# The first pair of heads in two half copies, a feature cast on ScalarE and 26 constant matmuls ahead of TensorE's queue

## The chip, the cores and the metric

One Trainium2 chip, one of its cores. The metric is the device time of one launch in microseconds (us), as the median of several runs; less is better. Engines are named as the profile names them: PE (TensorE; PEld for its weight loads), DVE (VectorE), ACT (ScalarE), POOL (GpSimd), SP (SyncE, which here only issues DMAs).

## The reference, cut to what matters

Attention with a feature map, for 8 batches, 8 heads, 576 tokens and a head width of 64, and then a dense mixture of 8 experts:

```
def phi(x):
    proj = np.einsum('bhsd,df->bhsf', x, w_phi)                  # 64 -> 128 features
    proj = proj - np.max(np.abs(proj), axis=-1, keepdims=True)
    return np.concatenate([np.exp(proj), np.exp(-proj)], axis=-1)
q_p, k_p = phi(q), phi(k)
kv  = np.einsum('bhsf,bhsd->bhfd', k_p, v)
num = np.einsum('bhsf,bhfd->bhsd', q_p, kv)
den = np.einsum('bhsf,bhf->bhs', q_p, np.sum(k_p, axis=2))[..., None] + 1e-06
x   = (num / den), as 4608 tokens x 512
P   = 8 rounds of row and column scaling of exp(x @ w_gate)
out = sum over e of P[:, e] * (relu(x @ w1[e]) @ w2[e])
```

The change lies in the first steps of the attention: bringing k and q of the first two heads into the layout in which `phi` is computed.

## The kernel before, in words

**Attention.** Heads are taken in pairs. For a pair, 512 of the 576 tokens are loaded as `acc` tiles (float32, 128 partitions); the remaining 64 tokens of a batch's heads, the "rest", are handled together (`rest_a`). In `pair_a` a pair of an early batch is turned on PE: four 128x128 transposes of k into one bank of PSUM, four of q into another (line 752), and each bank is copied as bfloat16 into the tile `qkT`: k's by DVE (line 756), q's by ACT (line 760). Then `tokens` projects k: four matmuls with 128 tokens each as weights and the feature matrix `wphi2` (256 columns: the 128 features of either head) as the moving operand. DVE takes the maximum of the absolute values (`m`, line 614), ACT the exponentials (`k`, line 618). `feature_rows` projects q the other way round with two matmuls of 512 columns, from which ACT makes `q`; another `tokens` on q yields q's maxima. After that come the sums over tokens (`kv`), numerators and denominators (lines 905 to 919), and the result is turned into `xT` (lines 934 and 937). Batches 0 and 1 are turned on PE, later ones by DMA.

**Experts.** From about 200 us on the rest of the kernel multiplies blocks of `xT` with the experts' weights (lines 1466, 1475, 1607), in an order written out by hand. The change touches nothing there.

**What sets the order of the work.** The kernel records its operations in a `Plan`: `pe(...)`, `act(...)`, `dve(...)`, `pool(...)` and `dma(...)` append one with a rough duration, what it reads and what it writes. `Plan.schedule` then plays all engines forward and gives each the operation that can start first, ties by the order of recording; buffers, among them the eight PSUM banks, are dealt out in that play. What comes out is one fixed list of instructions for each engine, and semaphores between them. An engine never passes over a waiting instruction. Lines 614, 618 and 622 are helpers that record maxima, exponentials and matmuls, so many operations carry these lines.

**The start.** Before the first pair can be projected, `wphi2` must stand: it holds the 64x128 matrix `w_phi` twice, at partitions 0 to 63 for the first head and 64 to 127 for the second, with zeros elsewhere. DVE clears it (line 1042); two DMAs, issued by ACT (lines 1035 and 1037), bring `w_phi` into both halves of `wphi_f`; DVE casts each half to bfloat16 as it lands (line 1044). SP issues the loads of k, q and v of the first pair, of k and q of the second, and of the rest (lines 544, 558 and 600). The tile `colw`, 128x128 ones, is set by DVE (line 1055) and used much later.

Of the kernel before, what the change touches and what calls it, by code (L numbers as in the profile page):

```python
# [349 lines left out]
def kernel(  # L350
# [11 lines left out]
    nc = tc.nc  # L362
# [26 lines left out]
    colw = const.tile([128, 128], BF16, name="colw")  # L389
# [5 lines left out]
    acc = [accp.tile([128, 4, DD], FP32, name=f"acc{g}", tag=f"acc{g}") for g in range(NA)]  # L395
# [3 lines left out]
    identf = a_in.tile([128, 128], FP32, name="identf")  # L399
    wgate_f = a_in.tile([128, NP, E], FP32, name="wgate_f")  # L400
    wphi_f = a_in.tile([128, DF], FP32, name="wphi_f")
    wphi2 = a_in.tile([128, 2, DF], BF16, name="wphi2")
# [10 lines left out]
    def pe(cols, fn, r=(), w=(), takes=()):  # L413
        plan.op("PE", max(cols / 2400.0 + 0.0025, 0.031), 0.22, fn, r, w, takes)

    def act(el, fn, r=(), w=()):
        plan.op("ACT", max(el / 1200.0 + 0.058, 0.107), 0.22, fn, r, w)

    def dve(el, fn, r=(), w=(), shared=False):
        plan.op("DVE", el / 960.0 + 0.07, 0.15, fn, r, w, shared=shared)  # L420

    def pool(el, fn, r=(), w=()):
        plan.op("POOL", el * 1.68e-3 + 0.13, 0.15, fn, r, w, shared=True)
# [4 lines left out]
    def dma(queue, nbytes, rate, fn, r=(), w=()):  # L428

        speed, unit = LINK.get(rate, (rate, 40))  # L430
        if nbytes == 2 << 20:
            speed, unit = 400, 150
        o = plan.op(queue, 0.8 if queue == "POOL" else 0.6, 0.0, fn, r, w, (), nbytes / speed)
        o.turn, o.unit = rate == 148, unit
# [71 lines left out]
    def new(tag):  # L506
        return R[tag].new()
# [28 lines left out]
    def load_qk(b, hh, nh, t, r=()):  # L536

        o = hh % 4
        keys = [o // 2] if nh == 2 else [0, 1]
        if b < 2:  # L540
            g = t["f"]
            for x, src in ((1, k), (0, q)):
                i = 2 * x + o // 2
                dma("SP", nh << 17, 320, lambda x=x, src=src, i=i: nc.sync.dma_start(
                    out=acc[g][:, i:i + nh // 2].rearrange("p a (h c) -> p (a h) c", h=2),
                    in_=src[b, hh:hh + nh, 0:SM].rearrange("h (p j) d -> p h (j d)", j=NJ)),
                    r, [("acc", g, 2 * x + n) for n in keys])
            return
        for x, src in ((1, k), (0, q)):
            dma("POOL", nh << 17, 230, lambda x=x, src=src: nc.gpsimd.dma_start(  # L550
                out=t["qk"]()[:, x, o:o + nh],
                in_=src[b, hh:hh + nh, 0:SM].rearrange("h (p j) d -> p h (j d)", j=NJ)),
                r, [(t["qk"], x, i) for i in keys])
# [67 lines left out]
    def mm(out_, lhsT, rhs, start, stop):  # L621
        nc.tensor.matmul(out_, lhsT=lhsT, rhs=rhs, start=start, stop=stop)  # L622

    def two(merged):

        if merged:
            b = new("P2")
            return [b], [lambda: b()[:, 0:512], lambda: b()[:, 512:1024]]
        b = [new("PP") for _ in range(2)]
        return b, b  # L630

    def tokens(pp, stat, n, r, takes=()):

        if not TI:
            for c in range(n):
                pe(256, lambda c=c: mm(pp[1][2 * c // n]()[:, 1024 // n * c % 512:][:, 0:256],
                                       stat(c), wphi2f, True, True),
                   r + ["wphi2"], [pp[0][2 * c // n * (len(pp[0]) - 1)]], takes)
            return

        def rows():
            for c in range(n):
                for x in range(2):
                    nc.tensor.matmul(pp[1][x]()[:, 128 * c:128 * c + 128],
                                     lhsT=stat(c)[64 * x:64 * x + 64],
                                     rhs=wphi[64 * x:64 * x + 64], start=True, stop=True)

        o = plan.op("PE", n * 0.056, 0.22, rows, r + ["wphi"], pp[0], takes)
        o.tiled = 1
# [18 lines left out]
    def rest_a(b, t):  # L668
# [25 lines left out]
        own = r["E"] + r["T"] + [m, r["r"], r["em"]]  # L694
        pp = two(RM)
        tokens(pp, lambda c: rT()[:, c, :], NP, [rT], own)
        if TI:
            mk = [(m, x) for x in range(2)]
# [43 lines left out]
    def pair_a(b, pr, t):  # L742

        h0 = (2 * pr) % 4
        s = {}
        if b < 2:
            g = t["f"]
            for x in (1, 0):
                ptr = new("PP")
                i = 2 * x + h0 // 2  # L750
                for c in range(4):
                    pe(128, lambda c=c, i=i, ptr=ptr: nc.tensor.transpose(  # L752
                        ptr()[:, c * 128:(c + 1) * 128], acc[g][:, i, c * 128:c * 128 + 128],
                        identf), [("acc", g, i), "identf"], [ptr])
                if x:
                    dve(512, lambda x=x, ptr=ptr: nc.vector.tensor_copy(
                        out=t["T"]()[:, x, 2 * h0:2 * h0 + 4, :].rearrange("p a b -> p (a b)"),
                        in_=ptr()), [ptr], [(t["T"], x, h0 // 2)])
                else:
                    act(512, lambda x=x, ptr=ptr: nc.scalar.copy(  # L760
                        out=t["T"]()[:, x, 2 * h0:2 * h0 + 4, :].rearrange("p a b -> p (a b)"),
                        in_=ptr()), [ptr], [(t["T"], x, h0 // 2)])

        def qkT(x, c, n):

            o = 2 * h0 + c
            return t["T"]()[:, x, o:o + n, :].rearrange("p a b -> p (a b)")
# [7 lines left out]
        own = s["E"] + s["T"] + [s["v"], em, m, s["r"]]  # L775
        at = (0, 2)

        def scores(x, pp):

            merged = (QM, KM)[x]  # L780
            for i, buf in enumerate(pp[0]):
                n = 1 + merged
                if TI or (GR and x == 0):
                    def src(buf=buf, n=n):
                        return buf().rearrange("p (h c f) -> p h c f", h=n, c=4)

                    def part(full, i=i, n=n):
                        return full.rearrange("p (c h) f -> p h c f" if len(full.shape) == 3
                                              else "p (c h) -> p h c", h=2)[:, i:i + n]
                else:  # L790
                    def src(buf=buf, n=n):
                        return buf().rearrange("p (c f) -> p c f", f=DF)

                    def part(full, i=i, n=n):
                        return full[:, 4 * i:4 * i + 4 * n]

                maxes(512 * n, lambda part=part: part(m()[:, at[x]]), src, [buf],
                      [(m, x, i), ("max", x, NP * b + pr)])
                if x == 1:
                    for y, sg in ((0, 1.0), (1, -1.0)):  # L800
                        exp(512 * n, lambda y=y, part=part: part(s["E"][y]()), src, sg,
                            [buf], [(s["E"][y], i)])
            return [(m, x, i) for i in range(2 - merged)]

        pk = two(KM)
        tokens(pk, lambda c: qkT(1, c, 1), 4, [(t["T"], 1, h0 // 2)], own)
        mk = scores(1, pk)
        pool(8, lambda: nc.gpsimd.tensor_scalar_mul(m()[:, 1], m()[:, 2], -1.0), mk, [(m, "neg")])
        exp(16, lambda: em(), lambda: m()[:, 1:3], 1.0, mk + [(m, "neg")], [em])
        pool(1024, lambda: nc.gpsimd.tensor_tensor(  # L810
            out=s["v"]()[:, :, :, 0:D],
# [219 lines left out]
    for b in range(2):  # L1031
# [4 lines left out]
        w=["wphi_f0"])  # L1036
    dma("ACT", 1 << 15, 100, lambda: nc.scalar.dma_start(out=wphi_f[64:128, :], in_=w_phi),
        w=["wphi_f1"])
    load_v(0, 0, 2, halves[0, 0])
    pool(300, lambda: make_identity(nc, identf), w=["identf"])  # L1040
    act(128, lambda: nc.scalar.copy(out=ident, in_=identf), ["identf"], ["ident"])
    dve(128, lambda: nc.vector.memset(wphi2, 0.0), w=["wphi2"])
    for i in range(2):
        dve(64, lambda i=i: nc.vector.tensor_copy(
            out=wphi2[64 * i:64 * i + 64, i, :], in_=wphi_f[64 * i:64 * i + 64, :]),
            [f"wphi_f{i}"], ["wphi2"])
    load_qk(0, 2, 2, halves[0, 0])
    load_rests(0, 1)
    load_v(0, 2, 2, halves[0, 0])
# [2 lines left out]
    for i in range(2):  # L1052
        dve(450, lambda i=i: nc.vector.memset(vrd[i], 0.0),
            w=[("vrd", i, h, *y) for h in range(2) for y in ((), (1,))])
    dve(128, lambda: nc.vector.memset(colw, 1.0), w=["colw"])
    dma("SP", 1 << 14, 50, lambda: nc.sync.dma_start(
        out=wgate_f, in_=moe_w_gate.rearrange("(c p) e -> p c e", p=128)), w=["wgate_f"])
    act(32, lambda: nc.scalar.copy(out=wgate, in_=wgate_f), ["wgate_f"], ["wgate"])
# [4 lines left out]
    def stage_a(i):  # L1063
        b, pr = i // 4, i % 4
        st[i], ms[i], qs[i] = pair_a(b, pr, halves[b, pr // 2])
# [993 lines left out]
```

## Time and profile before

| | |
|---|---|
| three runs | 1010.14, 1010.58, 1012.14 us; median 1010.58 |
| span of the profiled execution | 1008.8 us, 1.8 us less than the median |
| PE busy | 994.0 us |
| DVE busy | 898.6 us |
| ACT busy | 812.8 us |
| POOL busy | 447.6 us |

The span runs from the first to the last instruction of the program in one execution; the runs' times hold what lies around it too, and the profile tells no time of its own beside the span. A matmul's end in the profile is modelled, so the starts of matmuls say more than the sums of their durations. A row of the instructions in order of time has start and length in us, engine, line, operation, what is written from what, and in brackets the engine's idle time before it and what ended it. PEld rows often carry the wait of the matmul behind them.

### The profile page before, as it was taken

How to read it: one execution, taken by the hardware profiler on the slowest of the kernel's cores; microseconds unless marked ns; L12 is line 12 of the kernel's file. 1: busy time of each engine (PE TensorE's matmuls, PEld its weight loads, DVE VectorE, ACT ScalarE, POOL GpSimd, SP SyncE). 2: the span in 40 equal slices, each digit the busy share in tenths (PEclk: the TensorE clock that was granted, in tenths of full speed). 3: DMA queues.
4: the chain of work that ended last, by engine and by line, in shares of the span. 5: the costliest groups of instructions: out<-in, count | busy, mean ns of one | idle time of the engine just before them, and what ended most of it. 6: DMA issues, size and time to landing. Idle time of an engine off the chain costs nothing.

```text
span 1008.8 us, 23309 instructions
## 1 busy us (share of the span) xinstructions
PE 994.0 (99%) x8376; PEld 727.7 (72%) x8376; DVE 898.6 (89%) x1999; ACT 812.8 (81%) x1930; POOL 447.6 (44%) x514
## 2 busy tenths in 40 slices
PE   7899999999999999999999999999999999999998
PEld 5666666644566877777777877787778777787775
DVE  7999998987888998899989898989889988989886
ACT  7999999845979788878878788777887888778874
POOL 5778674400133344434444444444443444344443
PEclk9999999999999999999999999999999999999999
DMA  9999999181136423282327133632246222724653
GB/s 249 183 202 183 157 153 144 38 170 56 53 121 143 147 97 98 84 184 96 109 98 170 44 100 131 130 127 98 97 117 177 97 98 84 147 79 142 208 174 126
DMA packets 129748, 128.86 MB, mean 128 GB/s; under 512 B 55776, under 2 KB 98272, under 8 KB 129632
## 3 DMA queue, kind: packets, MB, share of 16 engines
q1 hardware_dynamic: 97680, 103.33, 36.3%
q0 software_dynamic: 31648, 23.86, 16.9%
q8 instruction: 65, 1.06, 0.5%
q14 instruction: 51, 0.42, 0.2%
q10 hardware_dynamic: 304, 0.20, 0.1%
HBM read 122.50 MB, written 19.53 MB: 141 GB/s over the span
## 4 chain that ended last, share of the span: by engine, by line
PE 92%; DVE 3%; ACT 2%; DMA 2%; issue 1%; POOL 0%; DVEq 0%
PE ps L1466 41%; PE ps L1475 20%; PE ps L622 17%; PE ps L1607 11%; PE ps L905 2%; DMA xi6t<-X 1%; DMA xi<-X 1%; PE ps L752 1%; ACT q L618 0%; DVE m L614 0%; ACT k L618 0%; DVE wx L614 0%; DVE X L1240 0%; DMA acc<-in_k_dram 0%; DVE hs L1676 0%
## 5 line engine op out<-in xcount | busy, mean ns | idle before, releaser
L1875 POOL TENSOR_TENSOR acc<-acc,hx 128x512 f32<-128x512 f32 x186 | 236.1, 1276 | 404.7 <-ACT hx L1872 135.0
L1466 PEld LDWEIGHTS <-hs 128*128 128x128 bf16 x1984 | 194.1, 98 | 46.4 <-issue 0.2
L1872 ACT ACTIVATE hx<-ps,P 128x256 f32<-128x256 f32 x372 | 158.9, 483 | 53.4 <-PE ps L1466 52.0
L1860 DVE SCALAR_TENSOR_TENSOR acc<-ps,P,acc 128x256 f32<-128x256 f32 x372 | 162.2, 478 | 30.2 <-PE ps L1466 28.2
L1475 PE MATMUL ps<-xT,T 128*128 128x512 bf16 x608 | 171.0, 379 | 0.0
L1466 PEld LDWEIGHTS <-hx 128*128 128x128 bf16 x1488 | 145.6, 98 | 24.9
L1466 PE MATMUL ps<-hx,hs 128*128 128x256 bf16 x992 | 144.3, 273 | 0.0
L1676 DVE CUSTOM_DVE_ANT_0 hs<-ps,U 128x512 bf16<-128x512 f32 x192 | 124.7, 684 | 11.3 <-PE ps L1475 6.6
L1607 PE MATMUL ps<-xT 128*128 128x256 bf16 x576 | 125.4, 272 | 0.0
L1475 PEld LDWEIGHTS <-T 128*128 128x128 bf16 x672 | 65.8, 98 | 40.6
L1682 ACT ACTIVATE hs<-ps 128x512 bf16<-128x512 f32 x96 | 55.9, 598 | 41.7 <-PE ps L1475 40.2
L1466 PE MATMUL ps<-wx,hs 128*128 128x256 bf16 x560 | 78.4, 273 | 0.0
L622 PE MATMUL ps<-w,hx 128*128 128x512 bf16 x288 | 73.0, 379 | 0.0
L622 PE MATMUL ps<-xT,w 128*128 128x512 bf16 x288 | 72.9, 379 | 0.0
L1466 PE MATMUL ps<-wx,hx 128*128 128x256 bf16 x496 | 72.3, 273 | 0.0
L1676 DVE CUSTOM_DVE_ANT_0 hs<-ps,X 128x512 bf16<-128x512 f32 x96 | 65.1, 684 | 7.8 <-PE ps L1607 6.9
L1466 PE MATMUL ps<-hx 128*128 128x256 bf16 x496 | 71.2, 273 | 0.0
L1607 PEld LDWEIGHTS <-xT 128*128 128x128 bf16 x576 | 56.3, 98 | 17.5
L1466 PE MATMUL ps<-w,hx 128*128 128x256 bf16 x432 | 62.2, 273 | 0.0
L614 DVE TENSOR_REDUCE m<-ps 128x4 f32<-128x512 f32 x88 | 58.8, 680 | 3.7 <-PE ps L622 1.9
L1672 ACT COPY X<-ps 128x512 f32<-128x512 f32 x96 | 58.6, 610 | 2.5 <-DVE ps L1650 2.5
L1466 PE MATMUL ps<-w,hs 128*128 128x256 bf16 x432 | 60.2, 273 | 0.0
(174 smaller groups left out, 2256.0 us busy)
## 6 DMA issues: line engine op xcount, KB each, us to landing
xT<-xi SPq DMA_DIRECT2D x48, 448.0 KB, 4.6
xT<-xd SPq DMA_DIRECT2D x72, 256.0 KB, 4.0
wx<-in_moe_w_dram POOLq DMA_DIRECT2D x8, 1024.0 KB, 11.2
v_m<-in_v_dram SPq DMA_DIRECT2D x15, 512.0 KB, 5.2
out_dram<-acc SPq DMA_DIRECT2D x14, 512.0 KB, 3.0
w<-in_moe_w_dram POOLq DMA_DIRECT2D x6, 1024.0 KB, 11.0
xT<-xp SPq DMA_DIRECT2D x24, 256.0 KB, 2.8
qk<-in_k_dram POOLq DMA_DIRECT2D x12, 256.0 KB, 5.4
```

What stands on the lines that cost most here:

```text
L614: dve(el, lambda: nc.vector.tensor_reduce(out=dst(), in_=src(), axis=AX.X, op=ALU.max, apply_absolute_value=True), r, w)
L622: nc.tensor.matmul(out_, lhsT=lhsT, rhs=rhs, start=start, stop=stop)
L905: pe(65, lambda j=j: nc.tensor.matmul(pn()[:, j * D1:j * D1 + D1], lhsT=s["T"][x]()[:, j % 2, 2 * h + j // 2, :] if j < 4 else r["T"][x]() ...
L1466: pe(256, lambda i=i, k=k, z=z: nc.tensor.matmul(bank()[:, 256 * i:256 * i + 256], lhsT=lhs(k, i), rhs=rhs(k), start=first and z, stop=k = ...
L1475: pe(512, lambda k=k: nc.tensor.matmul(bank().rearrange("p (a b) -> p a b", a=2), lhsT=lhs(k), rhs=rhs(k), start=first and k == 0, stop=k ...
L1607: pe(256, lambda: nc.tensor.matmul(halves_of(bank[q], n)(), lhsT=lhs(), rhs=t()[:, rhs, :], start=start, stop=True, skip_group_check=True) ...
L1672: act(512, lambda: nc.scalar.copy(out=flat(to[q])(), in_=bank[q]()), [bank[q]], [(to[q], 0), (to[q], 1)])
L1676: dve(515, lambda: nc.vector._custom_dve(ADD_SAT, out=out_(q, i, j), in0=bank[q]().rearrange("p (a b) -> p a b", a=2), in1=to[q](), s0=3.0 ...
L1682: act(512, lambda: nc.scalar.activation(out=out_(q, i, j), in_=bank[q]().rearrange("p (a b) -> p a b", a=2), func=ACT.Relu, bias=0.0, scal ...
L1860: dve(320, lambda n=n, ts=ts: nc.vector.scalar_tensor_tensor(out=acc[g][:, ts, 256 * j:256 * j + 256], in0=bank()[:, 256 * n:256 * n + 256 ...
L1872: act(370, lambda n=n: nc.scalar.activation(out=u()[:, n, :], in_=bank()[:, 256 * n:256 * n + 256], func=ACT.Copy, bias=0.0, scale=P[:, 4 ...
L1875: pool(695, lambda: nc.gpsimd.tensor_tensor(out=acc[g][:, 2 * i:2 * i + 2, 256 * j:256 * j + 256], in0=acc[g][:, 2 * i:2 * i + 2, 256 * j: ...
```

## The change

Three things are done, all in the first 10 us of the kernel.

1. For the first pair of the first batch, k's four transposes go into two banks, two in each. ACT copies the first two as one piece of 256 columns, DVE the last two. The projection of k names the half that it reads. The transposes and the copy of q, and all other pairs, are as before.
2. The second half of `wphi2` is cast by ACT instead of DVE.
3. `colw` is set first of all on DVE, and 26 matmuls of `colw` with itself (128 columns each) are recorded ahead of everything else on PE. They write a bank that nobody reads them from.

```
+                if x and not (b or pr):
+                    ph = new("PP")
+                    for n, f, to in ((0, act, ptr), (1, dve, ph)):
+                        for c in (2 * n, 2 * n + 1):
+                            pe(128, lambda c=c, i=i, to=to: nc.tensor.transpose(
+                                to()[:, c % 2 * 128:c % 2 * 128 + 128],
+                                acc[g][:, i, c * 128:c * 128 + 128], identf),
+                                [("acc", g, i), "identf"], [to])
+                        cp = nc.vector.tensor_copy if n else nc.scalar.copy
+                        f(256, lambda x=x, n=n, to=to, cp=cp: cp(
+                            out=t["T"]()[:, x, 2 * n:2 * n + 2, :].rearrange("p a b -> p (a b)"),
+                            in_=to()[:, 0:256]), [to], [(t["T"], x, 0, n)])
+                    continue
...
+    dve(128, lambda: nc.vector.memset(colw, 1.0), w=["colw"])
     dve(128, lambda: nc.vector.memset(wphi2, 0.0), w=["wphi2"])
-    for i in range(2):
-        dve(64, lambda i=i: nc.vector.tensor_copy(
-            out=wphi2[64 * i:64 * i + 64, i, :], in_=wphi_f[64 * i:64 * i + 64, :]),
-            [f"wphi_f{i}"], ["wphi2"])
+    idle = new("PP")
+    for i in range(26):
+        pe(128, lambda: mm(idle()[:, 0:128], colw, colw, True, True), ["colw"], [idle])
+    dve(64, lambda: nc.vector.tensor_copy(out=wphi2[0:64, 0, :], in_=wphi_f[0:64, :]),
+        ["wphi_f0"], ["wphi2"])
+    act(64, lambda: nc.scalar.copy(out=wphi2[64:128, 1, :], in_=wphi_f[64:128, :]),
+        ["wphi_f1"], ["wphi2"])
...
-    dve(128, lambda: nc.vector.memset(colw, 1.0), w=["colw"])
```

In the lists of instructions that come out, POOL and SP keep theirs, and DVE and ACT differ only in the operations named above. On PE, three things differ beside the 26: q's transposes of the first pair now also wait for an instruction of ACT, since they write the bank that ACT's half was read from; the second feature matmul of the first pair stands after the second pair's four transposes of k instead of before them; and four transposes of a later block (of batch 1) stand two groups of 65-column matmuls earlier. Further on, PSUM banks are dealt differently in the attention, so that some of its instructions wait for another engine than before; their order is the same.

More of the change, by code (lines that the diff above doesn't have):

```diff
@@ L630, in two, with tokens @@
         return b, b
-    def tokens(pp, stat, n, r, takes=()):
+    def tokens(pp, stat, n, r, takes=(), parts=False):
         if not TI:
@@ L637, in tokens @@
                                        stat(c), wphi2f, True, True),
-                   r + ["wphi2"], [pp[0][2 * c // n * (len(pp[0]) - 1)]], takes)
+                   ([(*r[0], c // 2)] if parts else r) + ["wphi2"],
+                   [pp[0][2 * c // n * (len(pp[0]) - 1)]], takes)
             return
@@ L805, in pair_a @@
         pk = two(KM)
-        tokens(pk, lambda c: qkT(1, c, 1), 4, [(t["T"], 1, h0 // 2)], own)
+        tokens(pk, lambda c: qkT(1, c, 1), 4, [(t["T"], 1, h0 // 2)], own, not (b or pr))
         mk = scores(1, pk)
```

## The prediction

> **What bounds the kernel now.** Read first: the page's head, then busy time by stretch (columns: length, then busy time and count of PE, PEld, DVE, ACT, POOL; granted clock; DMA share; GB/s).
>
> ```profile
> span 1008.8 us, 23309 instructions
> ...
> 5.00:10.00 5.00, 4.85 (x21) 3.02 (x21) 2.99 (x5) 3.23 (x7) 0.34 (x2) 1.00 1.15 219
> 10.00:15.00 5.00, 3.72 (x27) 2.24 (x25) 4.72 (x8) 4.72 (x11) 3.52 (x5) 1.00 0.98 301
> 15.00:20.00 5.00, 4.25 (x31) 2.73 (x29) 4.95 (x9) 5.00 (x17) 4.90 (x9) 1.00 1.26 291
> 20.00:30.00 10.00, 8.77 (x124) 6.49 (x125) 9.51 (x23) 9.84 (x26) 7.52 (x15) 1.00 1.34 262
> 30.00:40.00 10.00, 8.78 (x100) 6.50 (x99) 9.63 (x22) 9.93 (x25) 7.35 (x13) 1.00 1.31 174
> 40.00:50.00 10.00, 9.27 (x115) 6.23 (x114) 9.93 (x26) 10.00 (x28) 8.06 (x17) 1.00 1.31 157
> 50.00:75.00 25.00, 24.63 (x330) 17.33 (x328) 24.29 (x60) 24.20 (x60) 17.87 (x28) 1.00 1.12 200
> ```
>
> From 10 to 50 us ACT (39.5 of 40 us) and DVE (38.7 of 40) have no room; after 50 PE takes over (24.63 of 25). So whatever instant ACT and DVE reach at about 10 us is handed down, through engines that never pause, to the end. The change touches only what lies before 10 us. Next, the chain of waits there (start, length, what):
>
> ```profile
> 0.72 3.13 DMA acc<-in_k_dram
> ...
> 3.99 1.10 PE ps L752 x4
> ...
> 5.11 0.69 DVE qkT L756
> ...
> 5.83 0.24 DVE wphi L1044
> ...
> 6.11 1.86 PE ps L622 x6
> 7.97 1.05 PE ps L752 x4
> ...
> 9.04 0.98 PE ps L752 x4
> 10.02 0.23 PE ps L622 x2
> ...
> 10.28 0.68 DVE m L614
> ```
>
> k of the first pair lands at 3.85, is turned (3.99), copied (5.11), waits for the second feature cast (5.83), is projected (6.11); then the second pair's k and q are turned (7.97, 9.04). The chain calls 6.11 to 10 one unbroken run of PE, as if a gain at 6.11 passed straight through. The instructions in order of time, with the idle time before each, say otherwise:
>
> ```profile
> 4.86 0.72 PEld L752 LDWEIGHTS ps<-identf,acc 128*128 128x128 f32 x4 [0.19 <-DMA acc<-in_q_dram]
> ...
> 7.91 0.71 PEld L752 LDWEIGHTS ps<-identf,acc 128*128 128x128 f32 x4 [0.84 <-DMA acc<-in_k_dram]
> ...
> 9.04 0.71 PEld L752 LDWEIGHTS ps<-identf,acc 128*128 128x128 f32 x4 [0.42 <-DMA acc<-in_q_dram]
> ...
> 10.06 0.58 ACT L760 CAST qkT<-ps 128x512 bf16<-128x512 f32 x1 [0.25 <-PE ps L752]
> ```
>
> PE's weight loads for the second pair waited for landings: its k until 7.91, its q until 9.04. The change moves no DMA and reorders none on SP or ACT, so these two instants stay. They cap what a faster first pair can bring.
>
> **The change, part by part.** Durations are of the profiled execution; its span is 1008.8 us, the median of the three runs 1010.58, so 1.8 us lie around the span, and I add the same 1.8 behind.
>
> *Rate of PE.* Rows for it:
>
> ```profile
> 6.11 1.01 PE L622 MATMUL ps<-wphi,qkT 128*128 128x256 bf16 x4
> 6.92 1.06 PE L622 MATMUL ps<-qkT,wphi 128*128 128x512 bf16 x2
> 9.86 1.04 PE L622 MATMUL ps<-wphi,qkT 128*128 128x256 bf16 x8
> 20.29 0.61 PEld L622 LDWEIGHTS <-k 128*128 128x128 bf16 x16
> 20.34 0.68 PE L622 MATMUL ps<-v,k 128*128 128x65 bf16 x16
> 20.86 0.63 PE L752 MATMUL ps<-identf,acc 128*128 128x128 f32 x4
> ```
>
> Four 256-column matmuls took 1.01 us at 6.11, eight took 1.04 at 9.86: about 0.20 apart, then 0.11. The granted clock reads 1.00 in every stretch, so only durations show it. The turns at 9.04 are still slow (0.98 for four; 0.63 at 20.86). PE thus doubled between 9.04 and 9.86, say 9.8, which is 5.8 us after its first work at 3.99.
>
> *26 constant matmuls.* They need colw, whose memset now heads DVE's queue:
>
> ```profile
> 0.82 0.17 DVE L1042 MEMSET wphi<- 128x128 uint32 x1 [0.82 <-PEq L2043]
> ...
> 1.31 0.61 ACTq L1037 DMA_DIRECT2D wphi_f<-in_w_phi_dram  x1
> ...
> 3.25 0.30 ACT L1041 CAST ident<-identf 128x128 bf16<-128x128 f32 x1
> ...
> 4.20 0.22 DVE L1044 CAST wphi<-wphi_f 64x128 bf16<-64x128 f32 x1 [0.89 <-DMA wphi_f<-in_w_phi_dram]
> ...
> 13.99 0.66 ACT L618 ACTIVATE kr<-ps 128x256 bf16<-128x256 f32 x2
> ...
> 21.06 0.43 DVE L892 CAST kv<-ps 128x260 bf16<-128x260 f32 x1 [0.30 <-PE ps L622]
> ```
>
> colw is ready at 0.99; the first matmul starts at about 1.15 (0.05 for the wait, 0.1 for its weights). 128 columns slow is half of 256: 0.10 each, 2.6 us, done by 3.8. The other bound is 0.20 each, if the 26 weight loads don't hide: 5.2 us, done at 6.35. I take 0.10, since 16 loads (0.61) hid beside 16 matmuls (0.68) at 20.3. PE is then free when k lands, and the 26 cost nothing; the other memsets come 0.17 later, covered by DVE's 0.89 idle before its cast.
> The Trainium skill, "TensorE: Matmul & The Clock Gate", section "Part 1: The HAM clock gate", gives 107 ns from one cold 128x128x128 matmul to the next. By it the 26 end at 3.93, still before 3.96; no run here has such a matmul yet.
>
> *When PE gets fast.* Its work now starts 2.84 us earlier. With the same 5.8 us it doubles at 7.0: too late for the first pair, in time for the second. Bounds: 4.5 (all of pair one fast too) and 9.8 (nothing gained).
>
> *First pair, PE slow.* Turns of k start at 3.99 as before and come 0.21 to 0.23 apart; the second ends at 4.64. ACT copies its half in 0.38 (two 256-wide pieces take 0.66 above; bounds 0.30 to 0.40): 4.67 to 5.05. DVE's half follows the fourth turn, 5.11 plus 0.43: 5.54, where the whole copy ended at 5.80. The second feature cast leaves DVE; its data lands 3.7 us after the issue at 1.31,
>
> ```profile
> DMA to landing us min/median/max: 3.4/3.5/3.7
> ```
>
> that is at 5.02, and ACT, free at 5.05, casts until 5.35 (0.30 as for ident, 0.22 at least). Old end 6.07, so this is 0.7 us off the path.
> But a new wait: in the changed program the turns of q wait for ACT, because they write the bank that ACT's half is read from. They start at 5.08, not 4.86; behind them on PE stands all of pair one. Slow, they fill PE until about 5.96, and k's projection, ready at 5.56, starts there: 5.97 against 6.11. The gain is 0.14, and it would be 0.6 to 0.7 with PE fast.
>
> *Moved.* The second feature matmul of pair one now stands between the second pair's turns of k and of q. Its reader on ACT is
>
> ```profile
> 10.54 0.60 ACT L618 ACTIVATE q<-ps 128x512 bf16<-128x512 f32 x1
> ```
>
> With PE fast it runs at 8.35 to 8.6, between two landings; nobody is late. Four turns of a later block also move ahead of two groups of 65-column matmuls near 22 us (0.15 us of PE, while ACT sets the pace): nothing, bounds 0.15 either way.
>
> *Second pair, PE fast.* k's turns still start at 7.91 and q's at 9.04. q's take 0.63 and not 0.98, minus 0.35: the end is 9.67, not 10.02. Behind them, by the chain, DVE's m at 10.28 becomes 9.93, and ACT's copy at 10.06 becomes 9.70; ACT's own queue ended at 9.81 before (10.06 less 0.25 idle), less the 0.14 of pair one: 9.67, just in time. Both engines are 0.35 early as they enter the stretch without room.
>
> *Handed down?* DVE, ACT, POOL and SP keep their order from there on. The list of waits between 10 and 50 us has 35 groups, the first and the last of them
>
> ```profile
> PEld L622 <- issue: 3.2, 9, 0.6
> ...
> PE ps L678 <- DVE m L614: 0.2, 1, 0.2
> ```
>
> (total, times, longest), and none is for a DMA; the nearest, PE's turns of the rest rows,
>
> ```profile
> 11.02 0.42 PEld L678 LDWEIGHTS ps<-identf,acc 128*128 128x128 f32 x4 [0.41 <-DVE m L614]
> ...
> 12.08 0.68 DVE L683 CAST rT<-ps 128x512 bf16<-128x512 f32 x1
> ```
>
> ended on DVE. Their data may be late by up to 0.35 for an earlier PE, but the copy behind them on DVE starts a full microsecond later (12.08). I carry 0.35 whole; the lower bound is zero.
>
> **Sum:** 0 (26 matmuls) - 0.35 (turns of q at 9.04) + 0 (moves) = -0.35. Span 1008.45; time 1010.58 - 0.35 = **1010.2**. Pair one's own 0.14 to 0.7 adds nothing: the landing at 9.04 takes it.
>
> **Rivals.**
> *A: the clock was fast at 9.04 anyway* in the executions behind the median, though not in the profiled one. Then only ACT's 0.11 (9.81 to 9.70) is left: 1010.5. For: one profile shows one instant. Against: in it the doubling came 0.8 us too late.
> The skill's same section speaks for this: the activity window, about 3.4 us, is free-running and the warm-up differs between runs. By it the doubling before would fall between 7.4 and 10.8 (first full window after 3.99), in half the cases past 9.04; after, at 8.0 at the latest. By that rule, the trace (9.8, hence 0.35) is one draw.
>
> *B: slow at 7.9, and the moved feature matmul is in the way.* PE has little to do between 6 and 7.9 and may fall back or not yet have doubled. Then k's turns hold PE until 8.82, the feature matmul 0.43 more (1.06 less 0.63 for two), q's turns start at 9.25 and not 9.04, and k's and q's projections run slow: second one done at 10.73, DVE's m at 10.76, 0.48 late: **1011.1**, slower. It decides at 7.9: fast, it is nothing; slow, it is all of this. For: the more of pair one is done fast, the longer PE pauses before 7.9. Against: it paused later too and stayed at 0.11 ((0.61 - 0.27) / 3):
>
> ```profile
> 17.62 0.61 PE L622 MATMUL ps<-wphi,qkT 128*128 128x256 bf16 x4 [0.45 <-ACT qkT L760]
> ```
>
> Against it speaks also that section's table, by which only an idle window of about 3.4 us throttles; PE's longest pause here would be about 1 us.
>
> *C: the 26 hold the queue.* At 0.20 each they end at 6.35; PE is fast by then, ACT's half ends 7.13, q's turns 7.6, ACT's exponentials start 1.0 late and its copy at 10.86 instead of 10.06: +0.8, 1011.4. The point is (3.96 - 1.15) / 26 = 0.108 us each. The loads that hid at 20.3 speak against it.
>
> *D: drift.* The 26 take a PSUM bank, so later banks are dealt otherwise and some twenty waits of the attention stage name another engine. I give it up to 1 us either way: 1009.5 or 1011.5.
>
> **How the numbers follow.** Forecast (-0.2 to -0.5) 0.47; A 0.24; B 0.13; C 0.04; D 0.06 each way. The range, 1009.4 to 1011.3, takes in the forecast, A, B and half of D; the three runs before, 1010.14 to 1012.14, show that a median moves by some tenths by itself. 0.2% is 2.0 us, about what a measurement of this kernel can tell from no change: below 1008.6 or above 1012.6 needs twice of D, or D and C together: 0.05 each. Within: 0.90.
>
> **What would show it.** Right: 26 matmuls at 0.10 to 0.11 that end before 3.96; q's turns at 5.1 waiting for ACT; k's projection near 6.0; turns at 7.91 and 9.04 still waiting for DMA; q's four in 0.63; DVE's m at 9.9. Wrong: slow turns at 9.04 (B), k's turns after 4.1 (C), an m at 9.9 whose lead is gone by 50 us, or landings that have moved.

## The result, and the profile after

The changed kernel takes 1011.63 us (median of 16 runs, 1010.37 to 1014.03), the kernel before 1010.12 beside it (16 runs, 1009.27 to 1012.48): ratio 1.0016, 95% interval 1.0009 to 1.0023. It is slower by 1.5 us where I had forecast 0.35 us faster and a range that ended at 1011.3. The profiled execution of the changed kernel took 1013.65 us, 2 us more than its median, with this span:

```profile
span 1011.9 us, 23324 instructions
```

Its start, in order of time, answers to the rows of the prediction (new lines: L756 turns the halves of k and L761 copies them, L766 and L774 are the turns and q's copy of before's L752 and L760):

```profile
1.04 2.96 PE L622 MATMUL ps<-colw 128*128 128x128 bf16 x26 [1.04 <-DVE colw L1056]
...
3.79 1.06 PE L756 MATMUL ps<-identf,acc 128*128 128x128 f32 x4
...
4.46 0.37 ACT L761 CAST qkT<-ps 128x256 bf16<-128x256 f32 x1 [0.93 <-PE ps L756]
4.86 0.29 ACT L1063 CAST wphi<-wphi_f 64x128 bf16<-64x128 f32 x1
4.89 0.42 DVE L761 CAST qkT<-ps 128x256 bf16<-128x256 f32 x1 [0.79 <-PE ps L756]
4.95 0.57 PEld L766 LDWEIGHTS ps<-identf,acc 128*128 128x128 f32 x4 [0.50 <-ACT qkT L761]
...
5.60 0.60 PE L622 MATMUL ps<-wphi,qkT 128*128 128x256 bf16 x4
...
6.67 0.66 PE L766 MATMUL ps<-identf,acc 128*128 128x128 f32 x4
...
8.11 0.42 PEld L766 LDWEIGHTS ps<-identf,acc 128*128 128x128 f32 x4 [0.96 <-DMA acc<-in_q_dram]
...
9.03 1.89 DVE L614 TENSOR_REDUCE m<-ps 128x4 f32<-128x512 f32 x3 [0.82 <-PE ps L622]
```

Here almost everything came better than forecast. The 26 matmuls start at 1.04 and follow each other by 0.106 to 0.107 us; k's turns behind them start at 3.79. The projection of k runs at 5.60 and at full rate (0.60 for four, 1.01 before), and DVE's m of the second pair starts at 9.03, 1.25 us earlier than before.

So the loss lies later. I compared the start of each DVE instruction with that of the same one in the profiled execution of the kernel before (by order in DVE's list; the difference in us, at the time that the instruction had before):

```
at            11     31     72    113    236    285    900    930    960   1000
after      -1.25   0.11   0.79   0.78   1.97   2.19   1.84   2.42   3.33   3.02
```

The lead of 1.25 is gone by 31 us, and then time is lost in steps, the last of them at 920 to 960 us, where the change touches nothing. Some of the steps have owners. At 22 us PE waits for q of batch 1; at 280 us DVE, and near 924 and 957 us PE wait for transfers of x. The rows of the instructions in order of time, all of the changed kernel:

```profile
22.17 0.63 PE L766 MATMUL ps<-identf,acc 128*128 128x128 f32 x4 [0.98 <-DMA acc<-in_q_dram]
```

```profile
279.67 0.69 DVE L1257 TENSOR_TENSOR X<-xT 128x1024 bf16<-128x1024 bf16 x1 [0.74 <-DMA xi2t<-X]
```

and the waits of PE from 900 to 1000 us (total, times, longest), a list that is empty for PE in the kernel before:

```profile
PE ps L1492 <- DMA xT<-xp: 0.8, 1, 0.8
PE ps L1624 <- DMA xT<-xi: 0.4, 1, 0.4
```

The transfer behind the first of these is issued by SP in the same place of the same list as before. The view of DMA queues over just its flight, from issue to landing, tells what differs. Kernel before (952.8 to 956.2; packets, MB, share; then issues with KB and time to landing):

```profile
q1 hardware_dynamic: 300, 0.84, 72.5%
issues: line engine op xcount, KB each, median us to landing
...
xT<-xp SPq DMA_DIRECT2D x1, 256.0 KB, 3.4
```

Changed kernel (955.2 to 960.5):

```profile
q1 hardware_dynamic: 456, 1.40, 80.1%
q8 instruction: 1, 0.02, 1.1%
issues: line engine op xcount, KB each, median us to landing
...
xT<-xp SPq DMA_DIRECT2D x1, 256.0 KB, 5.3
```

There is one packet of a queue that I had passed over: q8, "instruction". The page has it in its list of queues, for the kernel before:

```profile
PE 994.0 (99%) x8376; PEld 727.7 (72%) x8376; DVE 898.6 (89%) x1999; ACT 812.8 (81%) x1930; POOL 447.6 (44%) x514
...
q8 instruction: 65, 1.06, 0.5%
```

There are 65 packets of 16 KB for PE's and PEld's 16752 instructions: one block for each 257.7. From the start of one of these packets to the next, PE and PEld start 144 to 327 instructions in the kernel before, 254 on the average, and the scatter does not add up over the 65. I read from this that q8 fetches PE's program during the run, in blocks of about 256 instructions, over the DMA engines that also move the data. And 26 matmuls with their 26 weight loads, put at the head, bring every later block 52 instructions nearer: each fetch comes earlier against the work, by a fifth of a block (a block lasts about 15 us). The Trainium skill, "Runtime: NRT & Kernel Launch", section "Instruction fetch mechanics", gives the same blocks of 256 instructions and calls the cost of crossing one "mostly hidden". For PE itself that agrees: from 400 to 700 us, with 18 fetches, the kernel before has PE busy for 100.00 of each 100 us. But by the rows above and the counts below, the transfers beside a fetch do wait.

That gave the theory to test. **F (fetch):** what costs is the number of instructions added, since it moves the fetches into flights of transfers that someone waits for. Rivals: **D**, the redealt banks and changed waits; **L**, the lead itself, by which transfers issued earlier meet other ones.

### The profile page after: what moved, and what is told of

Its sections match the earlier page's. It is cut to its first block, busy times and chain, and to the rows that moved or that the text cites. A ratio compares the mean times of both kernels' runs of the same rounds, so it can differ in the third digit from the quotient of the medians.

```text
span 1011.9 us, 23324 instructions
## 1 busy us (share of the span) xinstructions
PE 993.3 (98%) x8366; PEld 729.1 (72%) x8402; DVE 897.5 (89%) x1998; ACT 813.7 (80%) x1932; POOL 447.5 (44%) x514
## 4 chain that ended last, share of the span: by engine, by line
PE 69%; DMA 2%; DVE 1%; issue 0%; SPq 0%; ACT 0%; DVEq 0%; ACTq 0%
PE ps L1483 40%; PE ps L1492 18%; PE ps L1624 11%; DMA xi6t<-X 1%; PE ps L622 1%; DMA xT<-xp 1%; DMA xT<-xi 0%; DVE X L1257 0%; DVE acc L1877 0%; DVE hx L1257 0%; DVE hs L1547 0%; SPq L1241 0%; ACT hx L1889 0%; DVE w L1257 0%; DVE T L1257 0%
## 5 line engine op out<-in xcount | busy, mean ns | idle before, releaser
L622 PE MATMUL ps<-xT,w 128*128 128x512 bf16 x270 | 69.9, 379 | 0.7
L622 PE MATMUL ps<-w,hx 128*128 128x512 bf16 x274 | 69.9, 379 | 0.7 <-ACT q L618 0.2
```

## The experiments

**1 and 2: both kernels again, to see what belongs to an execution.**

> The kernel before once more, for the spread of its own waits. Scatter theory (losses behind 200 us are executions that differ, not the change): the landing of batch 1's q (before 20.64 us) and of the v tile that POOL waits for (before 57.92) differ by some tenths to 1 us, and the stretch from 200 us to the end by 1 to 2 us, between two profiles of one kernel. Theory that the change alone shifts them: both landings within 0.2 us of before, the span 1008.8 within 0.3.

> The changed kernel once more. Theory 1 (the lead meets a landing): again 0.4 to 1.3 us early from 10 to 20 us, PE again idle 0.5 to 1.0 us at about 21 us until batch 1's q has landed near 22.0, and at 30 us no lead is left (within 0.3 us of before). Theory 2 (redealt banks and moved transposes): the lead would go in small pieces over the whole stretch from 20 to 75 us instead. Scatter theory: the +0.7 at 62 to 72 us and the +1.2 at 215 to 230 us are not there again, or of another size.

Measured (before, beside the first four experiments: 1010.23): e1 1009.85 us (1009.61 to 1012.09), ratio 1.0001 [0.9992, 1.0009]; e2 1011.99 us (1011.44 to 1015.59), ratio 1.0023 [1.0008, 1.0038]. The difference repeats, and so do the steps at 285, 930 and 960 us (table below). The lead at 11 us does not: the kernel before reached that point 0.61 earlier in e1 than in its first profile. Neither expectation of e1 held whole: its span is 1.0 below the first one and POOL's v landed 1.0 earlier, so landings are not fixed, but behind 113 us the two executions differ by 0.4 only, not by 1 to 2. Of e2's, the lead of theory 1 came and shrank, but 0.70 of it was left at 31 us, and PE's wait at 21 us did not come.

**3: the 26 alone,** issued ahead of the planned list, so that banks, waits and order are those of before.

```
     def run(self, tc):
         done = self.schedule()
         with tc.manual_schedule():
+            self.first()
...
+    def first():
+        nc.vector.memset(colw, 1.0)
+        for i in range(26):
+            mm(ps[:, 3584:3712], colw, colw, True, True)
```

> The kernel before, its order and banks untouched, with colw set first and the 26 matmuls issued ahead of everything, outside of the planner. No halves, no cast on ACT, no moved instruction. Theory 1: a lead of 0.3 to 0.9 us at 10 us (transposes at full rate), gone at 21 to 23 us at the landing of batch 1's q; the time within 0.05% of before, or slower if the earlier loads collide. Theory 2: nothing is redealt, so the lead is kept and the time is 0.3 to 0.9 us (0.03 to 0.09%) lower.

Measured: 1011.9 us (1010.44 to 1016.88), ratio 1.0021 [1.001, 1.0033].

**4: everything but the 26.** The plan still holds them, so order, banks, halves and the cast on ACT are those of the changed kernel, but nothing is issued for them.

```
-        pe(128, lambda: mm(idle()[:, 0:128], colw, colw, True, True), ["colw"], [idle])
+        pe(128, lambda: None, ["colw"], [idle])
```

> The changed kernel with its order and its banks, but the 26 matmuls are not issued. Theory 1: with the first transposes slow and no lead worth the name (0 to 0.3 us at 12 us), loads are issued as before and the time is that of before within 0.1%. Theory 2: the banks and the moved transposes are there, so it is as slow as the changed kernel (0.1 to 0.2% over before).

Measured: 1009.72 us (1009.08 to 1010.97), ratio 0.9994 [0.9986, 1.0003]. With the third this settles which part it is: the 26 alone cost what the whole change costs, and the rest of the change, its banks and waits included, costs nothing that shows. D falls.

**5 to 8: same early work with fewer instructions, and same instructions with little work.** The first three are edits of the third kernel's `first`, the fourth puts the six wide matmuls into the changed kernel.

```
-        for i in range(26):
-            mm(ps[:, 3584:3712], colw, colw, True, True)
+        wide = colw.unsqueeze(1).to_broadcast([128, 4, 128])
+        for i in range(6):
+            mm(ps[:, 3584:4096].rearrange("p (a b) -> p a b", a=4), colw, wide, True, True)
```

> The kernel before, with six matmuls of 512 columns issued ahead of PE's list in place of the 26 of 128 columns: about the same 2.6 us of early work for PE and the same early doubling, but 12 more PE instructions instead of 52. Theory F (fetch): each instruction added ahead shifts the 16 KB blocks in which PE's instructions are fetched (256 instructions each), and a fetch that falls into a transfer that PE waits for delays it. By it the blocks move by 12/256 of some 15.5 us, 0.7 us, instead of 3.1: the fetches near 277 and 958 us stay clear of the transfers before them, the losses of the 52 at 113, 280 and 958 us are not there, the one at 924 may be; the early lead of some tenths stays: 1009.7 us (1009.3 to 1010.4). Theory L (lead): the early start of PE itself does it, since transfers issued earlier meet others later: the same losses as with 26, 1011.9 us.

Measured (before beside these four: 1010.17): 1010.18 us (1009.62 to 1011.55), ratio 1.0001 [0.9992, 1.001]. It lies in F's range; the early lead that was to stay did not show in its profile (0.14 late at 11 us).

```
+        wide = colw.unsqueeze(1).to_broadcast([128, 2, 128])
+        for i in range(13):
+            mm(ps[:, 3584:3840].rearrange("p (a b) -> p a b", a=2), colw, wide, True, True)
```

> The kernel before, with 13 matmuls of 256 columns ahead: the same 2.7 us of early work, 26 more PE instructions. Theory F: blocks 1.5 us earlier; the fetches near 277 and 923 us then lie inside the transfers issued at 273.7 and 920.6, the one near 958 us does not reach the one issued at 952.8: losses of about 0.4 each at 280 and 924 us, none at 958: 1010.7 us (1010.0 to 1011.2). Theory L: 1011.9 us, with the same losses as 26.

Measured: 1011.11 us (1009.83 to 1013.9), ratio 1.0011 [1.0003, 1.002]. The size came as expected by F, the place not: nothing at 280 and 924 us, where the fetches began 3.0 and 3.6 us after the issue and the transfers landed on time, but 1.47 us between 101 and 105. It comes from a transfer of qkT that, issued at 92.71, took 5.64 us with a fetch 3.0 us after its issue (4.28 in e1, without one), and POOL waited for it:

```profile
POOL qk L551 <- DMA qkT<-qk: 1.8, 1, 1.8
```

```
         for i in range(26):
-            mm(ps[:, 3584:3712], colw, colw, True, True)
+            mm(ps[:, 3584:3592], colw, colw[:, 0:8], True, True)
```

> The kernel before, with 26 matmuls of 8 columns ahead: 52 more PE instructions as in the change, but half the early work or less (26 times some 0.05 us), so that the clock doubles later or as before. Theory F: the fetches fall as with the 26 of 128 columns, and so do the losses at 113, 280, 924 and 958 us: 1012.0 us (1011.3 to 1012.6). Theory L: without an early doubling as before: 1010.1 us (1009.6 to 1010.6).

Measured: 1012.53 us (1011.4 to 1014.34), ratio 1.0026 [1.0015, 1.0037]: the slowest of all, with no early work to speak of (26 in 0.7 us) and no early doubling. Its waits of PE from 900 to 1000 us are for the same two transfers as in the changed kernel, in other shares:

```profile
PE ps L1608 <- DMA xT<-xi: 0.9, 1, 0.9
PE ps L1476 <- DMA xT<-xp: 0.4, 1, 0.4
```

```
-        pe(128, lambda: mm(idle()[:, 0:128], colw, colw, True, True), ["colw"], [idle])
+        pe(128, lambda i=i: i < 6 and mm(idle()[:, 0:512].rearrange("p (a b) -> p a b", a=4),
+                                         colw, cw4, True, True), ["colw"], [idle])
```

> The changed kernel (its order, its banks, the halves and the cast on ACT) with six matmuls of 512 columns in place of the 26 of 128. Theory F: as the run without the 26, 1009.7, with some tenths of early lead on top: 1009.4 us (1009.0 to 1010.2), faster than both kernels. Theory L: 1011.9 us as the changed kernel.

Measured: 1009.59 us (1008.63 to 1012.17), ratio 0.9998 [0.9989, 1.0007]. With six wide matmuls for the 26 the change costs nothing. Each set against its own measurement of before, it stands at -0.58 (1009.59 less 1010.17) and the changed kernel at 1.76 (1011.99 less 1010.23): 2.3 us better than the changed kernel; that it beats the kernel before is not shown. L falls: six wide matmuls do the same 2.7 us of early work and lose nothing, 26 small ones lose without it.

**9: the same 52 instructions late.** Nothing at the head; 26 small matmuls, overwritten by the real one behind them, stand near 930 us.

```
+    def few(out_, lhsT, rhs, start, **kw):
+        few.n += 1
+        if few.n > 3529 and start and not few.done:
+            few.done = True
+            for i in range(26):
+                nc.tensor.matmul(out_[:, 0:8], lhsT=lhsT, rhs=rhs[:, 0:8],
+                                 start=True, stop=True, skip_group_check=True)
+        return nc.tensor.matmul(out_, lhsT=lhsT, rhs=rhs, start=start, **kw)
```

> The kernel before with nothing at the head; 26 matmuls of 8 columns stand near 930 us instead, ahead of a group of line 1466 in PE's list. PE is busy there, so they cost their own time, 26 by 0.027 us (the spacing of the 26 small ones in the run before) = 0.7 us. Theory F (fetch): all blocks up to 930 us stay, so there is no loss at 280 and at 924 us; the block that ends near 958 us moves ahead by 52 instructions, into the transfer issued near 952.8, which lands 1 to 2 us later and costs PE 0.5 to 0.9 at 956: 1010.15 + 0.7 + 0.55 = 1011.4 us (1011.0 to 1012.0). Theory H (something at the head, at the start of the kernel): the 0.7 alone, no wait at 956: 1010.85 us (1010.4 to 1011.3).

Measured (before beside these four: 1010.31): 1011.17 us (1010.51 to 1013.42), ratio 1.0013 [1.0004, 1.0022]. The median is in both ranges; the trace decides. The offset is 0.24 up to 930 us, 0.82 after the small matmuls (0.58, where 0.7 was expected), and 1.48 from 958 on: 0.66 at the one transfer in which F puts the fetch, none at 285 and 924. The only wait of PE from 900 to 1000 us, and the DMA queues from 953.6 to 958.7:

```profile
PE ps L1486 <- DMA xT<-xp: 0.5, 1, 0.5
```

```profile
q1 hardware_dynamic: 436, 1.33, 76.4%
q8 instruction: 1, 0.02, 1.1%
issues: line engine op xcount, KB each, median us to landing
...
xT<-xp SPq DMA_DIRECT2D x1, 256.0 KB, 5.0
```

So the place can be chosen: the extra instructions act on the next fetches behind them, wherever they stand.

**10 to 12: more instructions, up to a whole block.** As the seventh, with 52, 104 and 128 small matmuls (`range(52)` and so on).

> The kernel before with 52 matmuls of 8 columns at the head (104 more PE instructions, done by 2.5 us, before k lands). Theory F: the blocks move by 104 of 256 instructions, 6 us; the fetches then start before the transfers at 273.7, 920.6 and 952.8 us are issued, and near 101 before that of 103.0: no loss at these four places, 1010.2 us (1009.6 to 1011.0), though another transfer, not seen so far, may be hit in their place. Theory N (the loss grows with the number of instructions added, as from 12 to 26 to 52): twice the 2.4 us of the 26 small ones, 1014.9 us.

> 104 matmuls of 8 columns at the head (208 more PE instructions, done by 3.85 us, as k lands). Theory F: blocks moved by 208 of 256, that is 48 short of a whole block: the four transfers are clear, 1010.2 us (1009.6 to 1011.0), with the same reserve on others. Theory N: four times 2.4, 1019.7 us.

> 128 matmuls of 8 columns at the head: 256 more PE instructions, a whole block, done by 4.5 us, so that k's turns start 0.5 us later, which the landings of the second pair at 7.9 and 9.04 us cover for the most part. Theory F: every later fetch falls at the same place of the work as in the kernel before (one block earlier in number), and all the losses of the 26 are gone although five times as many instructions are added: 1010.4 us (1009.7 to 1011.0), waits for transfers as before. Theory N: 1021.9 us. If the number does not matter but that any were added: 1012.0 us.

Measured: 52: 1011.65 us (1010.16 to 1013.86), ratio 1.0015 [1.0006, 1.0024]; 104: 1010.84 us (1010.15 to 1013.54), 1.001 [1.0001, 1.002]; 128: 1010.68 us (1010.14 to 1011.94), 1.0006 [0.9997, 1.0014]. N falls at once: the last has five times the instructions of the seventh kernel and stands 0.37 above before, not 2.36. With a whole block added, the fetches fall where they fell before, and the transfer of the ninth kernel is quick again (DMA queues from 953.65 to 957.2, 128 small ones):

```profile
q1 hardware_dynamic: 311, 0.88, 71.8%
issues: line engine op xcount, KB each, median us to landing
...
xT<-xp SPq DMA_DIRECT2D x1, 256.0 KB, 3.5
```

The 52 missed F's range by 0.65, although their trace has no wait at 285 and 957 us, as F says. That one execution was the quickest of its eleven, so two more executions of it were profiled.

> The kernel with 52 small matmuls once more, for another profiled execution: the profiled one of the run before was the fastest of its eleven (1010.16, median 1011.65) and shows no loss that would explain the median. Theory F: the 1.3 us above the kernel before appear as a wait for a transfer in the attention (before 226 us, above all the wait of POOL for v at 59 us or that of PE and POOL near 100 us), with a block fetch inside that transfer's flight; at 280 and 956 us nothing, as before. Theory S (the loss is spread, not tied to transfers): the offset against the kernel before grows in small steps everywhere, or in the stage after 226 us.

> The same kernel and the same two theories, a second execution, since the profiled ones differ at the start by some tenths. Theory F: a step before 226 us at a transfer with a fetch in flight, none at 280 and 956 us. Theory S: small steps everywhere.

Measured: 1011.31 and 1012.33 us (one run each; before 1010.09, one run). Both expectations missed. There is no late step at a transfer and no spread: the three executions differ at 13 us (-0.46, 0.18, 1.39 against before), gain 0.3 to 0.5 by 236 us, and lose nothing behind it but 0.1 to 0.2 at 924. It is the start that varies: in the last one PE waited for k of the second pair until 8.70, and was still slow:

```profile
8.70 2.16 PE L753 MATMUL ps<-identf,acc 128*128 128x128 f32 x8 [1.35 <-DMA acc<-in_k_dram]
```

Eight turns in 2.16 us, where four took 0.66 at 6.67 in the changed kernel. Whether the 52 make this start more frequent was not tried, so the median of this kernel, 1.34 above before, stays unexplained by F.

**All profiled executions side by side:** the offset of DVE's instructions against the first profile of before, in us, at the time that they had there.

```
at                        11     31     72    113    236    285    900    930    960   1000
52 instructions more ahead of all fetches:
  after                -1.25   0.11   0.79   0.78   1.97   2.19   1.84   2.42   3.33   3.02
  e2_after             -1.62  -0.70   0.05   0.04   0.24   0.62   0.26   0.62   1.58   1.27
  e3_26_outside        -0.53  -0.14  -0.15   0.34   0.11   0.36   0.37   0.77   1.25   1.26
  e7_26_tiny           -0.30   0.13   1.53   1.52   1.92   2.19   2.02   3.11   3.67   3.67
none or a whole block:
  e1_before            -0.61  -0.62  -0.63  -0.63  -1.17  -1.17  -1.00  -1.01  -1.01  -1.01
  e4_no26              -0.23  -0.18  -0.17  -0.17  -0.29  -0.29  -0.61  -0.61  -0.61  -0.92
  e12_128_tiny          0.83   0.83   1.06   1.04   0.89   0.90   0.87   0.87   0.87   0.87
other numbers:
  e5_6_wide (12)        0.14   0.14   0.13   0.12   0.31   0.30   0.32   0.32   0.32   0.32
  e8_6_wide_plan (12)  -1.80  -0.72  -0.73  -0.75  -1.00  -0.98  -1.28  -1.28  -1.29  -1.60
  e6_13_mid (26)        0.02   0.02   0.01   1.50   1.24   1.24   1.12   1.12   1.12   1.13
  e11_104_tiny (208)   -0.31  -0.32  -0.32  -0.33  -0.14  -0.12   0.15   0.15   0.14   0.14
  e9_late (52 at 930)   0.03   0.03   0.53   0.52   0.40   0.39   0.24   0.24   1.48   1.47
```

From 236 us on, the kernels of the first group lose at 285, 930 and 960 (0.22 to 0.38, 0.36 to 1.09 and 0.48 to 0.96), the others nowhere but where a fetch was put.

And the three transfers behind these steps, issue to landing in us, in all 16 profiled executions (the three of the 52 small ones among them):

```
transfer, issued near    with a fetch in its flight       without
xi2t<-X       274 us     3.88 3.92 3.93 4.05  (4)         1.99 to 2.00  (12)
xT<-xi        921 us     4.58 4.63 4.78 5.29  (4)         3.61 to 4.08  (12)
xT<-xp        953 us     4.83 4.92 5.01 5.26 5.31  (5)    3.16 to 3.66  (11)
```

"In its flight" is 0.9 to 3.2 us after the issue; a fetch that began within 0.4 us of the landing or behind it counts as without. (This line was drawn with the times known; the nearest case is the sixth kernel's xT<-xp, which had a fetch 3.03 us after its issue and landed after 3.16.) There is no overlap. The qkT issued near 91 us, as a fourth, agrees in the main: 4.26 to 4.35 us in the 8 executions without a fetch in its flight, 4.30 to 6.09 in the 8 with one. Nor is it a mere coincidence in time: xi2t is 144 packets, 128 of 2048 bytes and 16 of 4. Before, all had ended by 275.38, within 1.7 us of the issue. In each of the four slow cases exactly 9 of the 144 ended after the fetch's packet did: in the third kernel the fetch ran from 274.73 to 276.25, 135 packets ended by 275.48, and the last nine from 276.47 to 277.28. The nine are eight of 2048 bytes and one of 4: a sixteenth of the transfer each time. With the page's 16 DMA engines this fits one engine held by the 16 KB block, and a transfer that waits for its slowest sixteenth; the trace does not name a packet's engine, so that last step is argued.

## Why the prediction was wrong, point by point

- **The 26 matmuls.** The step that failed is "PE is then free when k lands, and the 26 cost nothing". Their time was right: 0.106 to 0.107 apart, where I took 0.10. The 107 ns of the Trainium skill, "TensorE: Matmul & The Clock Gate", section "Part 1: The HAM clock gate", agree with that. PE was not quite free when k landed: by the trace k landed at 3.60 and 3.53 in the two profiles after, with the 26 running until about 3.8, and the first turn started 0.19 and 0.26 behind the landing, against 0.14 before and in e1. That is a tenth of a microsecond, covered by later landings. The loss lies elsewhere: I counted only the time of PE. That 52 instructions in front of 16752 shift the fetches of the rest was in no term. The term should have been about +1.7: with no fetch hit e4 stands at -0.51 (1009.72 against 1010.23), and with the 26 alone e3 at +1.67. In the traces the three late transfers make 1.15 of it in e3 (0.26 + 0.41 + 0.48) and 1.70 in e2 (0.38 + 0.36 + 0.96); of the rest in e3, 0.49 lies between 101 and 107 us, behind the transfer of the sixth kernel: qkT, issued at 91.10, took 6.09 instead of 4.28 with a fetch 4.1 us after its issue, and POOL waited 0.8 for it.
- **When PE gets fast:** I said 7.0, with 4.5 as the early end. In the first profile after, q's turns at 4.98 change rate in their middle; in e2 it was about 6.6. The kernel before was fast by 7.58 in e1 (four turns in 0.66), against 9.8 in its first profile: rival A was true of some executions.
- **The first pair:** q's turns waiting for ACT at 4.95 (said 5.08) and ACT's half of 0.37 (said 0.38) came as worked out; k's projection at 5.60 and not 5.97, since PE was fast by then.
- **"These two instants stay":** they don't, even without a change. k and q of the second pair were waited for until 7.91 and 9.04 in the first profile before, 7.58 and 8.75 in e1, 6.67 and 8.11 after. So one profile was too little for a cap, and the lead of 1.25 in the changed kernel is in part such luck.
- **"Handed down? I carry 0.35 whole":** wrong too, though it could not have decided the sign. I read that no wait from 10 to 50 us was for a DMA, but a transfer that was in time by little shows no wait. The load of q that SP issued at 9.44 before landed at 15.01 there, at 14.60 in the first profile after, 14.85 in e2 and 14.71 in e8, hardly earlier. PE's turns of it could start no sooner than 14.70, 14.95 and 14.84: at 17 us the leads of 1.25, 1.62 and 1.80 are 0.94, 0.69 and 0.83. In the first profile after, batch 1's q, which landed at 20.64 before without a wait, landed at 22.04, and PE waited 0.98 for it at 22.17; that took the rest. I had given the four turns that were moved there 0.15 at most.
- **Rivals:** C did not occur in the size that I gave it (the 26 stay under 0.108 each). D was the wrong drift: e4 has all the redealt banks and costs nothing. B's mechanism showed itself harmlessly in e4, where PE was slow until 9.2 and the feature matmul held q's turns from 8.96 to 9.19. None of my rivals had a cost that lay outside the stage of the change, and that is why the range ended at 1011.3.
- **Open:** a step of 0.5 to 1.4 between 31 and 72 us, where POOL waits for a v, is in after, e2, e7 and also in e9. In the first three a fetch began 2.2 to 2.3 us before that v landed, in e9 0.4 us; but its flight scatters anyhow (8.3 to 9.8 us in these four, 7.1 to 8.0 in four others with a fetch late in it, 5.1 to 5.7 in three with an early one, 6.7 to 8.1 in five with none), so whether the fetch plays a part is not shown. And the growth by 1.2 at 215 to 236 in the first profile after is in no other in that size; its cause was not found. How much of the median each late transfer makes was not measured one by one.

## What to carry to other kernels

Instructions that fill idle time of an engine are not free because the engine is idle: here they shifted the blocks in which its whole later program is fetched, and a fetch takes 0.9 to 1.7 us for the most part, in which a transfer can be held up. Fill with few large instructions instead of many small ones, and when a small change at the head moves time near the end, look at the instruction queues in the flights of the transfers that are waited for. Where a program's late transfers have no slack, a number of instructions that is harmless in one place of 256 is not in another, so a difference of 0.2% between two versions may be this alone.

## What the runs showed of the hardware

- The 16 KB packets of the queue q8 came one for about 256 instructions of PE (257.7) and took 0.9 to 1.7 us for the most part; one such packet made a 256 KB transfer land after 3.9 instead of 2.0 us.
- Small matmuls did not bring the full rate early. Six matmuls of 512 columns ending near 3.8 us had PE at full rate for k's turns at 3.93 (four in 0.63); behind 104 small ones, which follow each other from 1.0 to 3.9 us but stream 8 columns each, PE was still slow at 8.73 (four loads in 0.71, against 0.42 at full rate) and fast by 9.55. The start of the full rate differs between executions (9.8 and at the latest 7.58 in two of the kernel before), so two alone would prove little; but in all six profiles with small matmuls at the head k's projection was still slow (four in 1.01), and in five of the six with wide ones or the 26 of 128 columns it was fast (0.60; 1.00 in e2). The instructions in order of time, first of the six wide (issued alone), then of the 104 small:

```profile
3.93 0.63 PE L753 MATMUL ps<-identf,acc 128*128 128x128 f32 x4 [0.15 <-DMA acc<-in_k_dram]
```

```profile
8.73 0.71 PEld L753 LDWEIGHTS ps<-identf,acc 128*128 128x128 f32 x4 [0.45 <-DMA acc<-in_q_dram]
```

- Matmuls of 8 columns, each with a load of the same 128x128 tile, followed each other by 0.026 to 0.027 us on a slow PE, so 128 of them cost 3.4 us.
